# The decoding's loads and stores moved from SyncE's queue to ScalarE's, with other tile counts

## The chip, the cores and the metric

The kernel runs on one core of one Trainium2 chip. The metric is the device time of one execution in microseconds (us). The kernel before was timed three times; the median is 1176.22 us.

## What is computed

Three stages follow each other. The first is causal attention with a decay per position, for 4 batches of 8 heads, 576 positions and 64 channels each:

```python
scores = scale * np.matmul(q, k.transpose(0, 1, 3, 2))
log_f = np.log(np.clip(f, 0.0001, 1.0))
cum = np.cumsum(log_f, axis=-1)
decay = cum[:, :, :, None] - cum[:, :, None, :]
scores = np.where(causal, -1000000000.0, scores + decay)
attn = np.exp(scores - np.max(scores, axis=-1, keepdims=True))
attn = attn / (np.sum(attn, axis=-1, keepdims=True) + 1e-09)
x = np.matmul(attn, v)
```

The heads side by side give 2304 tokens of 512 channels. Two layers of three weights each follow, with 1536 inner channels: `x1 = ((x @ w_a) * (x @ w_b)) @ w_out`, and then, after a normalization of x1 by its root mean square and a gain, `(silu(xn @ w_gate) * (xn @ w_val)) @ w_out2`. The weights are given in double precision.

## The kernel before

**The tiling.** The tokens are cut into four chunks, one for each batch; a chunk has two column halves of 256 to 320 tokens. Eight phases (`PHASES`, line 33) run a layer on a chunk. A phase has 36 weight granules (24 of the two input weights, 12 of the output weight); a granule is 128 x 512 weights, and for each half it gives one block of 12 matmuls (lines 584 to 586), since each weight and each activation is held as a high and a low part and three products are added up. A block of 288 columns takes about 1.6 us.

**The decoding.** The first time that a granule is used (`weights`, line 478), its 64-bit words are loaded into a tile `raw` (512 KB, line 509); ScalarE or GpSimd takes the upper word into `w32` (lines 514 and 516), VectorE fixes two bit fields (lines 520 and 526) and joins them (line 530, the last reader of `raw`), ScalarE makes the high part (line 485, `high`), GpSimd the low part (line 488, `low`), and the result, a tile `w` of 512 KB, is used and also stored into `wd` in device memory (line 535, `save`). There are 72 granules. Whenever a granule is used again, the stored form is loaded (line 494, 251 times). Before the change there are two `raw` tiles, so a raw load waits until the join of the granule two places earlier is done.

**The attention** is woven between the weight blocks. For each pair of heads `head` (line 1049) loads q, k, two rows each of decay sums (`aux`) and the values (`vr`, two loads); that is twelve transfers a pair. Then come the scores (lines 1108 and 1130), their maximum with the mask on VectorE (line 770), exp on ScalarE (line 777), transposes on TensorE (line 813), the copy of the transposed tile `pt` on ScalarE (line 1197), and the value products (line 1168).

**What sets the order.** `Plan` records every step as a node with an engine, a cost, a priority and its dependencies, simulates the engines (`order`, line 213), and writes the instructions in the order of its simulated starts. On the chip every engine runs its own list strictly in that order, each instruction with its waits. All transfers before the change are issued by SyncE (`SP`), whose list is one queue; a transfer that must wait for its tile holds up those behind it. The tiles rotate: a tile of a kind with n buffers waits until the users of the one n places earlier are done. The gate tiles are `a` (line 605), also used for the squares and for the outputs.

Of the kernel before, what the change touches and what calls it, by code (L numbers as in the profile page):

```python
# [13 lines left out]
I64 = mybir.dt.int64  # L14
# [44 lines left out]
QUIET = 9000  # L59

NORM_AT, NORM_STEPS = 6, (6, 10)
W_BUFS, W32_BUFS, A_BUFS, BP_BUFS = 5, 3, 4, 4
S_BANKS, T_BANKS, PV_BANKS, M_BANKS = 2, 1, 1, 4
P_BUFS, PT_BUFS = 3, 4


def mm(n):
# [9 lines left out]
def turn_cost(k, n):  # L77

    return k * (57 if n <= 64 else 109) - (50 if n > 64 else 0)


def act(n, psum=False):
    return (51 if psum else 93) + n / 1.2
# [60 lines left out]
class Plan:  # L144
# [7 lines left out]
    @staticmethod  # L152
    def latency(a, b):

        if a == SP:
            return 980
        if a == b:
            return {PE: 0, POOL: 0, DVE: 128}.get(a, 128)
        return 200 if a == PE else 230 if b == PE else 170 if b == POOL else 140

    def __init__(self):
        self.nodes, self.writer, self.readers, self.rings = [], {}, {}, {}
# [50 lines left out]
    def order(self):  # L213
# [23 lines left out]
        while len(done) < len(self.nodes):  # L237
            best = None
            for e, ns in cand.items():
                pick = None  # L240
                for n in ns:
                    t = max(free[e], n.ready)
                    if shared(n, e):
                        t = max(t, port[other[e]])
                    if pick and (t, n.prio) >= pick[0]:
                        continue
                    ok = True
                    if isinstance(n.eng, tuple):
                        ends_ = [
                            max(free[x], n.ready, port[other[x]] if shared(n, x) else 0) + c + (PEN if x == DVE else 0)  # L250
                            for x, c in zip(n.eng, n.cost)
                        ]
                        ok = ends_[n.eng.index(e)] == min(ends_)
                    for b in n.allocs if ok else ():
                        ring, i = self.rings[b.tag], turn[b.tag]
                        if ring[i] is not b:
                            ok = False
                            break
                        if i >= b.bufs:
                            ends = [u.end for u in ring[i - b.bufs].users]  # L260
                            if None in ends:
                                ok = False
                                break
                            t = max(t, max(u.end + self.latency(u.eng, n.eng) for u in ring[i - b.bufs].users))
                    if not ok:
                        continue
                    key = (t, n.prio)
                    if pick is None or key < pick[0]:
                        pick = key, n
                if pick and (best is None or pick[0][0] < best[0][0]):  # L270
                    best = *pick, e
# [14 lines left out]
            n.end = free[n.eng] = t + cost * (2 if n.eng == PE and t < self.COLD else 1)  # L286
            if shared(n, n.eng):
                port[n.eng] = n.end + 60
            if n.eng == SP:
                n.end = dma_free = max(t + 1150, dma_free) + n.bytes / 360  # L290
            done.append(n)
            for o in n.outs:
                o.waiting -= 1
                to = o.eng[0] if isinstance(o.eng, tuple) else o.eng
                o.ready = max(o.ready, n.end + self.latency(n.eng, to))
                if not o.waiting:
                    offer(o)
        done.sort(key=lambda n: n.start)
# [4 lines left out]
class Kernel:  # L303
# [119 lines left out]
    def weave(self):  # L423
# [10 lines left out]
        for p in range(np_):  # L434
            self.T.append([t])
            c = PHASES[p][1]
            for x, s in zip(extra[p], (s for _, subs in self.steps(p) for s in subs)):
                t += 12 * mm(size(c, s)) + x
                self.T[-1].append(t)
        self.x_parts, self.ab_blocks, self.decoded = {}, {}, set()  # L440
        self.plan_boot()
        self.op(
            DVE, dve2(128),
# [28 lines left out]
    def source(self, m, j):  # L472
        if j < 2 * FT:
            return self.w[m][j % 2][j // 2]
        j -= 2 * FT
        return self.w[m][2][j // 3, j % 3]

    def weights(self, m, j, t, start=0):
# [19 lines left out]
        self.decoded.add((m, j))  # L498


        raw = self.tile([128, 512], "raw", 2, I64)
        i32 = self.tile([128, 512], "w32", W32_BUFS, I32)

        def words(dtype, n):
            x = raw.tile.bitcast(dtype).rearrange("p (n t) -> p n t", t=n)
            return [x[:, :, i] for i in range(n)]

        def load(x):
            nc.sync.dma_start(x, self.source(m, j))

        def rebase(by, x):
            x, y = x.bitcast(F32), words(F32, 2)[1]
# [19 lines left out]
            )  # L532

        def save():
            nc.sync.dma_start(self.wd[m][j], flat(w.tile))

        op(SP, 480, load, writes=[raw], prio=t - 14000, nbytes=524288, start=start)
        op((ACT, POOL), (act(512) + 50, pool1(512)), rebase, reads=[raw], writes=[i32], prio=t - 8500)
        op(DVE, dve_words(512), last_bits, writes=[raw], prio=t - 8000, port=True)
        op(DVE, dve_words(512), sign, writes=[raw], prio=t - 7500, port=True)  # L540
        op(DVE, dve(512), join, reads=[raw], writes=[i32], prio=t - 7000, port=True)
        op(ACT, act(512), high, reads=[i32], writes=[(w, 0)], prio=t - 6000)
        op(POOL, pool2(512), low, reads=[i32, (w, 0)], writes=[(w, 1)], prio=t - 5500)
        op(
            SP, 480, save, reads=[(w, 0), (w, 1)], writes=[("wd", m, j)], prio=t - 4000, nbytes=524288,
        )
        return w

# [500 lines left out]
    def head(self, c, h, q0, t, sf):  # L1049
# [16 lines left out]
        top, dt, aux, at = (66, F32, self.aux32, (0, 1)) if sf else (68, F32R, self.aux, (0, 2))  # L1066
        qb, kb = (self.tile([top, S], x + "b", 2, dt) for x in "qk")
        qr, kr = (qb, kb) if sf else (self.tile([64, S], x, 1) for x in ("qr", "kr"))
        vr = self.tile([128, 5, D], "vr", 4)
        load(256 * (S - q0), lambda: qr.tile[0:64, q0:], self.qT[g, :, q0:], writes=[(qr, 0)], dt=15000)  # L1070
        load(147456, lambda: kr.tile[0:64], self.kT[g], writes=[(kr, 0)], dt=15000)
        for x, i in zip((qb, kb), at):
# [177 lines left out]
```

## Time and profile before

| | us |
|---|---|
| median of three runs (1173.39 to 1176.52) | 1176.22 |
| profiled execution | 1176.44 |
| its span, first to last instruction | 1174.6 |
| TensorE busy | 1146.0 |
| VectorE / ScalarE / GpSimd busy | 635.3 / 498.7 / 193.8 |

The span is one execution seen by the profiler. PE is TensorE, DVE VectorE, ACT ScalarE, POOL GpSimd, SP SyncE; SPq is SyncE's queue, where a row is the issue of a transfer and not the transfer itself. The granted clock is the share of 2.4 GHz at which TensorE was allowed to run; at the lower level of 1.2 GHz it reads 0.5, and a stretch that holds both reads in between. Idle time is put down to what ended it.

### The profile page before, as it was taken

What the parts mean: (1) busy time and instruction counts of PE and PEld (TensorE: products, weight loads), DVE (VectorE), ACT (ScalarE), POOL (GpSimd) and SP (SyncE); (2) the same over time, 40 slices, a digit from 0 to 9 for tenths busy, and PEclk for the clock granted to TensorE, in tenths of its full rate; (3) what the DMA queues carried; (4) which work ended last, traced back from release to release, by engine and by line L of the source; (5) the groups of instructions that cost most, each with busy time, mean ns of one, the idle gap of its engine ahead of it and who ended that gap; (6) DMA issues with size and microseconds to landing.
All of it is one profiled execution on the core that took longest, in us unless ns stands there. A gap on an engine that the chain in (4) does not pass through costs nothing.

```text
span 1174.6 us, 22748 instructions
## 1 busy us (share of the span) xinstructions
PE 1146.0 (98%) x8752; PEld 1087.2 (93%) x8752; DVE 635.3 (54%) x1654; ACT 498.7 (42%) x1272; POOL 193.8 (17%) x198
## 2 busy tenths in 40 slices
PE   8999999999899999999999999999999999999998
PEld 7666889989789999998999999999999999999998
DVE  7988857878886348897233148632132057303420
ACT  7676556656554445545223244533222134202220
POOL 2323304442323020444100010110000000000000
PEclk9999999999889999999999999999999999999999
DMA  7677686578499454567755444444555455565553
GB/s 200 237 246 257 235 316 212 198 237 320 147 335 323 146 158 139 201 225 248 235 172 159 144 155 148 137 149 152 176 172 166 161 163 165 171 200 169 164 170 119
DMA packets 76800, 229.81 MB, mean 196 GB/s; under 512 B 11444, under 2 KB 22212, under 8 KB 76660
## 3 DMA queue, kind: packets, MB, share of 16 engines
q1 hardware_dynamic: 76692, 228.36, 59.0%
q8 instruction: 69, 1.13, 0.4%
q14 instruction: 39, 0.32, 0.1%
HBM read 185.19 MB, written 43.13 MB: 194 GB/s over the span
## 4 chain that ended last, share of the span: by engine, by line
PE 72%; DVE 5%; DMA 4%; ACT 2%; issue 1%; POOL 1%; SPq 0%; ACTq 0%; POOLq 0%; DVEq 0%
PE m L584 22%; PE m L586 22%; PE m L585 21%; PE pv L1168 2%; PE t L813 2%; PE s L1108 2%; DMA raw<-wv 1%; DVE raw L526 1%; DVE w L530 1%; DMA w<-wd 1%; DMA raw<-wg 1%; DVE raw L520 1%; DMA raw<-wo 1%; PE s L1130 1%; DVE P L770 1%
## 5 line engine op out<-in xcount | busy, mean ns | idle before, releaser
L584 PE MATMUL m<-x,w 128*128 128x288 f32 (+2 forms) x1536 | 467.6, 304 | 4.0 <-DMA w<-wd 4.0
L586 PE MATMUL m<-x,w 128*128 128x288 f32 (+2 forms) x1536 | 456.6, 297 | 0.5 <-POOL w L488 0.5
L585 PE MATMUL m<-x,w 128*128 128x288 f32 (+2 forms) x1536 | 455.7, 297 | 0.0
L584 PEld LDWEIGHTS m<-x,w 128*128 128x128 f32 x1536 | 291.7, 190 | 11.6 <-DMA w<-wd 5.0
L585 PEld LDWEIGHTS m<-x,w 128*128 128x128 f32 x1536 | 291.8, 190 | 1.9 <-issue 1.0
L586 PEld LDWEIGHTS m<-x,w 128*128 128x128 f32 x1536 | 291.4, 190 | 1.1 <-POOL w L488 0.9
L584 PE MATMUL m<-g,w 128*128 128x288 f32 (+2 forms) x768 | 230.9, 301 | 0.0
L586 PE MATMUL m<-g,w 128*128 128x288 f32 (+2 forms) x768 | 227.1, 296 | 2.2 <-POOL w L488 2.2
L585 PE MATMUL m<-g,w 128*128 128x288 f32 (+2 forms) x768 | 226.5, 295 | 0.0
L626 DVE TENSOR_TENSOR a<-m,a 128x288 f32<-128x288 f32 (+2 forms) x192 | 88.0, 459 | 141.1 <-PE m L586 132.7
L642 ACT ACTIVATE g<-a 128x288 fp32r<-128x288 f32 (+2 forms) x192 | 84.9, 442 | 173.9 <-DVE a L626 173.5
L584 PEld LDWEIGHTS m<-g,w 128*128 128x128 f32 x768 | 144.7, 188 | 2.4 <-issue 2.1
L586 PEld LDWEIGHTS m<-g,w 128*128 128x128 f32 x768 | 144.4, 188 | 2.6 <-POOL w L488 2.6
L585 PEld LDWEIGHTS m<-g,w 128*128 128x128 f32 x768 | 144.7, 188 | 0.2
L608 ACT ACTIVATE a<-m 128x288 f32<-128x288 f32 (+2 forms) x192 | 78.2, 407 | 133.2 <-PE m L586 132.9
L488 POOL TENSOR_TENSOR w<-w,w 128x512 fp32r<-128x512 f32 x72 | 98.2, 1365 | 183.2 <-ACT w L485 157.7
L645 DVE TENSOR_TENSOR g<-a,g 128x288 fp32r<-128x288 f32 (+2 forms) x185 | 95.2, 515 | 59.5 <-ACT g L642 59.2
L777 ACT ACTIVATE P<-P,mn 128x512 f32<-128x512 f32 (+4 forms) x128 | 76.4, 598 | 57.4 <-DVE mn L770 56.4
L615 DVE SCALAR_TENSOR_TENSOR a<-a,m 128x288 f32<-128x288 f32 (+1 forms) x96 | 43.3, 454 | 96.8 <-ACT a L608 96.6
L770 DVE CUSTOM_DVE_ANT_0 P<-s,mask 128x512 f32<-128x512 f32 (+4 forms) x128 | 62.6, 501 | 42.2 <-PE s L1108 34.1
L1197 ACT ACTIVATE pt<-t 128x512 f32<-128x512 f32 (+4 forms) x144 | 63.9, 444 | 50.1 <-PE t L813 49.8
L813 PE MATMUL t<-ident,P 128*128 128x128 f32 (+1 forms) x376 | 67.7, 281 | 7.8 <-ACT pt L1197 5.2
(106 smaller groups left out, 1170.5 us busy)
## 6 DMA issues: line engine op xcount, KB each, us to landing
w<-wd SPq DMA_DIRECT2D x251, 512.0 KB
wd<-w SPq DMA_DIRECT2D x72, 512.0 KB
raw<-wo SPq DMA_DIRECT2D x24, 512.0 KB
raw<-wa SPq DMA_DIRECT2D x12, 512.0 KB
raw<-wb SPq DMA_DIRECT2D x12, 512.0 KB
raw<-wg SPq DMA_DIRECT2D x12, 512.0 KB
raw<-wv SPq DMA_DIRECT2D x12, 512.0 KB
vr<-vA SPq DMA_DIRECT2D x32, 128.0 KB
```

What stands on the lines that cost most here:

```text
L488: nc.gpsimd.tensor_tensor(out=w.tile[:, 1, :], in0=i32.tile.bitcast(F32), in1=w.tile[:, 0, :].bitcast(F32), op=ALU.subtract)
L584: nc.tensor.matmul(o, w.tile[:, 0, wc], xh, start=kt == 0, stop=False)
L585: nc.tensor.matmul(o, w.tile[:, 0, wc], xl, start=False, stop=False)
L586: nc.tensor.matmul(o, w.tile[:, 1, wc], xh, start=False, stop=kt == last)
L608: ACT, act(n, 1), lambda x: nc.scalar.activation(x[:, :n], acc.tile[:, :n], func, scale=scale),
L626: nc.vector.tensor_tensor(out=a.tile[:, :n], in0=acc.tile[:, :n], in1=a.tile[:, :n], op=ALU.mult)
L642: nc.scalar.activation(out(0), x(), AF.Copy, **({} if scale is None else {"scale": scale}))
L645: self.engine(by).tensor_tensor(out=out(1), in0=x(), in1=out(0).bitcast(F32), op=ALU.subtract)
L770: nc.vector.tensor_tensor_reduce(out=p.tile[:n, i * w : i * w + w], in0=s[i].tile[:n, :w], in1=masks[i][:n], scale=-0.125, scalar=mn.tile[ ...
L777: nc.scalar.activation(o, o, AF.Exp, bias=mn.tile[:n, len(s) - 1 : len(s)], scale=-1.0, accum_out=x[:n])
L813: nc.tensor.transpose(ps.tile[:w, c : c + n], p.tile[:n, i * 128 : i * 128 + w], self.ident[:n, :n])
L1197: ACT, act(m, 1), lambda *_: self.nc.scalar.activation(x.tile[:rows, :m], ps.tile[:rows, :m], AF.Copy),
```

## The change

The 72 raw loads and the 72 stores are issued by ScalarE instead of SyncE. In the planner they are nodes of ScalarE with a cost of 120 ns (`DMA_ACT`), and their end is still reckoned as a transfer's. A raw load is made dependent on the `high` step of the granule three places earlier, which is on the same engine and comes after the join. There are three `raw` tiles instead of two, and three instead of four of `a`, `pt` and `vr`. As the planner's inputs differ, it writes other orders for all engines. The lines of the changed file are 8 to 12 higher: 502 is 494 of before, 518 is 509, 544 is 535, 493 is 485, 596 to 598 are 584 to 586, 620 is 608, 789 is 777, 800 is 788, 825 is 813, 1074 is 1062, 1120 is 1108, 1180 is 1168, 1209 is 1197.

```diff
-W_BUFS, W32_BUFS, A_BUFS, BP_BUFS = 5, 3, 4, 4
+RAW_BUFS, W_BUFS, W32_BUFS, A_BUFS, BP_BUFS = 3, 5, 3, 3, 4
...
-P_BUFS, PT_BUFS = 3, 4
+P_BUFS, PT_BUFS, VR_BUFS = 3, 3, 3
...
+DMA_ACT = 120
...
+    @staticmethod
+    def source(n):
+        return SP if n.bytes else n.eng
...
-            t = max(t, max(u.end + self.latency(u.eng, n.eng) for u in ring[i - b.bufs].users))
+            t = max(t, max(u.end + self.latency(self.source(u), n.eng) for u in ring[i - b.bufs].users))
...
-            if n.eng == SP:
+            if n.bytes:
                 n.end = dma_free = max(t + 1150, dma_free) + n.bytes / 360
...
-                o.ready = max(o.ready, n.end + self.latency(n.eng, to))
+                o.ready = max(o.ready, n.end + self.latency(self.source(n), to))
...
-        self.x_parts, self.ab_blocks, self.decoded = {}, {}, set()
+        self.x_parts, self.ab_blocks, self.decoded, self.highs = {}, {}, set(), []
...
-        raw = self.tile([128, 512], "raw", 2, I64)
+        raw = self.tile([128, 512], "raw", RAW_BUFS, I64)
...
         def load(x):
-            nc.sync.dma_start(x, self.source(m, j))
+            nc.scalar.dma_start(x, self.source(m, j))
...
         def save():
-            nc.sync.dma_start(self.wd[m][j], flat(w.tile))
-
-        op(SP, 480, load, writes=[raw], prio=t - 14000, nbytes=524288, start=start)
+            nc.scalar.dma_start(self.wd[m][j], flat(w.tile))
+
+        op(
+            ACT, DMA_ACT, load, writes=[raw], prio=t - 14000, nbytes=524288, start=start,
+            after=self.highs[-RAW_BUFS:][:1] if len(self.highs) >= RAW_BUFS else [],
+        )
...
-        op(ACT, act(512), high, reads=[i32], writes=[(w, 0)], prio=t - 6000)
+        self.highs.append(op(ACT, act(512), high, reads=[i32], writes=[(w, 0)], prio=t - 6000))
...
         op(
-            SP, 480, save, reads=[(w, 0), (w, 1)], writes=[("wd", m, j)], prio=t - 4000, nbytes=524288,
+            ACT, DMA_ACT, save, reads=[(w, 0), (w, 1)], writes=[("wd", m, j)], prio=t - 4000, nbytes=524288,
         )
...
-        vr = self.tile([128, 5, D], "vr", 4)
+        vr = self.tile([128, 5, D], "vr", VR_BUFS)
```

**SyncE, at granule 12 of the second chunk's phase** (`wd0_12` is its stored form; qr and kr are head loads, raw a granule to decode). Before:

```order
L1062 DMA qb803_4162<-aux_136 4x576
L1062 DMA kb804_4183<-aux_136 4x576
L1062 DMA qb810_4190<-aux_136 4x576
L1062 DMA kb811_4194<-aux_136 4x576
L1062 DMA qr812_4272<-qT 64x576
L1062 DMA kr813_4276<-kT 64x576
L509 DMA raw1122_4302<-wv 128x512
L494 DMA w1109_4305<-wd0_12_150 128x1024
```

Now:

```order
L1074 DMA qb803_4159<-aux_136 4x576
L1074 DMA kb804_4171<-aux_136 4x576
L1074 DMA qb810_4195<-aux_136 4x576
L1074 DMA kb811_4200<-aux_136 4x576
L502 DMA w1109_4210<-wd0_12_150 128x1024
L1074 DMA qr812_4285<-qT 64x576
L1074 DMA kr813_4305<-kT 64x576
L502 DMA w1117_4308<-wd0_13_151 128x1024
```

The load of granule 12 stood behind qr, kr and a raw load; now it stands ahead of qr and kr, and the raw load is gone from this queue.

**TensorE, a little later** (s are scores of a head pair, t transposes of its first softmax). Before:

```order
L1108 MATMUL s827_4406<-ka809_4185,qa808_4165 128x128
L1108 MATMUL s827_4406<-kb804_4183,qb803_4162 128x128
L1108 MATMUL s831_4413<-ka816_4323,qa815_4309 128x128
L1108 MATMUL s831_4413<-kb811_4194,qb810_4190 128x128
L1108 MATMUL s840_4427<-ka809_4185,qa808_4165 128x256
L1108 MATMUL s840_4427<-kb804_4183,qb803_4162 128x256
L1108 MATMUL s844_4432<-ka816_4323,qa815_4309 128x256
L1108 MATMUL s844_4432<-kb811_4194,qb810_4190 128x256
L813 MATMUL t824_4453<-ident_96,P819_4402 128x128 x4
```

Now:

```order
L1120 MATMUL s827_4498<-ka809_4186,qa808_4161 128x128
L1120 MATMUL s827_4498<-kb804_4171,qb803_4159 128x128
L1120 MATMUL s831_4504<-ka816_4369,qa815_4349 128x128
L1120 MATMUL s831_4504<-kb811_4200,qb810_4195 128x128
L596 MATMUL m1132_4515<-x100_120,w1128_4467 128x288
L597 MATMUL m1132_4515<-x110_124,w1128_4467 128x288
L598 MATMUL m1132_4515<-x100_120,w1128_4467 128x288
```

Before, eight score matmuls and then the transposes follow each other; now two weight blocks of granule 15 come after the first four (the three rows of m1132 repeat, and m1133 follows), and the loads' earlier places put six blocks of granules 12 to 14 ahead of s817, where there were two.

**ScalarE, in the first stage, at the second head pair** (`pt114` and `pt115` are copies of transposed tiles for TensorE; the names in brackets are the semaphores that an instruction waits for, DMAHW0 to 7 those of transfers). Before:

```order
L788 ACTIVATE P111_798<-P111_798,sm113_846 128x576 [waits DVE_49,Activation_49]
L485 ACTIVATE w542_880<-w32544_815 128x512 [waits DMAHW5_49,DVE_49]
L1181 ACTIVATE x000_112<-pv102_858 128x128 [waits PE_49]
L608 ACTIVATE a537_886<-m536_833 128x256
L788 ACTIVATE P124_848<-P124_848,sm126_856 128x384 [waits DVE_49,Activation_49]
L1197 ACTIVATE pt114_903<-t116_889 128x512 [waits PE_49]
L514 ACTIVATE w32553_942<-raw552_875 128x512 [waits DMAHW6_49,Pool_49]
L1197 ACTIVATE pt115_946<-t117_927 64x128 [waits PE_49]
L485 ACTIVATE w547_951<-w32549_872 128x512 [waits DMAHW7_49,DVE_49]
```

Now:

```order
L544 DMA wd0_7_145<-w547_897 128x1024 [waits DMAHW3_49,Pool_49]
L518 DMA raw561_942<-wa 128x512 [waits DMAHW6_49]
L620 ACTIVATE a546_948<-m545_913 128x256 [waits PE_49]
L1209 ACTIVATE pt114_952<-t116_936 128x512 [waits PE_49]
L493 ACTIVATE w551_955<-w32553_849 128x512 [waits DMAHW0_49,DVE_49]
L800 ACTIVATE P124_926<-P124_926,sm126_931 128x384 [waits DVE_49,Activation_49]
L518 DMA raw566_982<-wb 128x512 [waits DMAHW3_49]
L1209 ACTIVATE pt115_987<-t117_967 64x128 [waits PE_49]
L789 ACTIVATE P133_984,sm135_993<-P133_984,mn134_985 128x512 [waits DVE_49]
L544 DMA wd0_8_146<-w551_955 128x1024 [waits DMAHW6_49,Pool_49]
```

Three of the moved issues stand among the softmax and decoding steps. The load `raw566` waits for DMAHW3, whose user before it is the store `wd0_7`, issued four computing steps and one load earlier, and the copy `pt115` stands behind it.

## Rows read from the trace of the kernel before

**Rows 1.** The page's parts 1 and 2: busy time by engine; granted clock in 40 slices (tenths).

```profile
PE 1146.0 (98%) x8752; PEld 1087.2 (93%) x8752; DVE 635.3 (54%) x1654; ACT 498.7 (42%) x1272; POOL 193.8 (17%) x198
...
PEclk9999999999889999999999999999999999999999
```

**Rows 2.** Busy time by stretch: us, then each engine's busy us (instructions), clock, DMA share, GB/s.

```profile
0.00:560.00 560.00, 534.47 (x4054) 481.77 (x4055) 424.59 (x1102) 324.03 (x831) 177.56 (x178) 0.98 0.68 231
```

**Rows 3.** The same view in stretches of 10 us.

```profile
110.00:120.00 10.00, 9.19 (x59) 5.90 (x57) 9.02 (x25) 6.87 (x20) 3.16 (x3) 0.83 0.67 234
...
130.00:140.00 10.00, 9.65 (x60) 8.50 (x61) 7.81 (x18) 4.67 (x11) 3.23 (x3) 0.83 0.59 221
...
300.00:310.00 10.00, 7.88 (x70) 7.47 (x68) 7.69 (x20) 6.62 (x17) 5.74 (x8) 0.99 0.45 133
310.00:320.00 10.00, 7.45 (x35) 7.02 (x35) 8.34 (x20) 3.59 (x9) 0.36 (x1) 0.67 0.34 115
320.00:330.00 10.00, 7.81 (x41) 5.97 (x42) 7.62 (x23) 6.05 (x17) 2.54 (x2) 0.50 0.81 279
```

**Rows 4.** TensorE in order of time: start us, length us, line, out<-in, [idle before <-releaser].

```profile
311.15 0.61 PE L584 MATMUL m<-x,w 128*128 128x288 f32 x1 [3.28 <-DMA w<-wd]
...
319.00 0.33 PE L1108 MATMUL s<-ka,qa 128*128 128x128 f32 x1 [0.90 <-DVE mn L770]
...
322.80 1.12 PE L813 MATMUL t<-ident,P 128*128 128x128 f32 x4 [0.82 <-ACT P L788]
...
327.95 0.61 PE L584 MATMUL m<-x,w 128*128 128x288 f32 x1
```

**Rows 5.** SyncE's queue in order of time (same columns).

```profile
298.26 0.29 SPq L1062 DMA_DIRECT2D kb<-aux  x1
303.14 0.47 SPq L1062 DMA_DIRECT2D qr<-qT  x1
304.40 0.47 SPq L1062 DMA_DIRECT2D kr<-kT  x1
305.40 0.36 SPq L509 DMA_DIRECT2D raw<-wv  x1
305.82 0.42 SPq L494 DMA_DIRECT2D w<-wd  x1
...
320.52 0.33 SPq L509 DMA_DIRECT2D raw<-wg  x1
320.90 0.90 SPq L494 DMA_DIRECT2D w<-wd  x2
```

**Rows 6.** VectorE in order of time, around 300 to 326 us (same columns).

```profile
304.70 0.68 DVE L530 SCALAR_TENSOR_TENSOR w<-w,raw 128x512 int32<-128x512 int32 x1
...
319.80 0.69 DVE L530 SCALAR_TENSOR_TENSOR w<-w,raw 128x512 int32<-128x512 int32 x1
```

**Rows 7.** TensorE's waits: engine line <- releaser: us in total, times, longest us.

```profile
PE t L813 <- ACT pt L1197: 5.2, 8, 1.5
PE m L584 <- DMA w<-wd: 4.0, 3, 3.3
PE m L586 <- POOL w L488: 2.7, 3, 1.4
```

**Rows 8.** SyncE's issues of the stores (line 535): durations in ns, min/median/max.

```profile
L535 SPq DMA_DIRECT2D wd<-w x72: 319/320/1170, 21.0 to 560.2; - x72
```

**Rows 9.** SyncE's waits (columns as TensorE's waits).

```profile
SPq L535 <- POOL w L488: 105.3, 57, 6.0
...
SPq L494 <- DMA wd<-w: 7.9, 3, 4.8
```

**Rows 10.** ScalarE in order of time (columns as TensorE's).

```profile
309.87 0.66 ACT L514 ACTIVATE w<-raw 128x512 f32<-128x512 f32 x1 [1.64 <-DMA raw<-wv]
```

**Rows 11.** ScalarE's groups up to 560 us: busy us, mean ns, idle before.

```profile
L485 ACT ACTIVATE w<-w 128x512 fp32r<-128x512 f32 x72 | 45.1, 627 | 22.7 <-DVE w L530 13.5 <-PE m L586 5.9 <-issue 1.6
```

**Rows 12.** GpSimd's groups (same columns).

```profile
L488 POOL TENSOR_TENSOR w<-w,w 128x512 fp32r<-128x512 f32 x72 | 98.2, 1365 | 183.2 <-ACT w L485 157.7 <-issue 10.5 <-PE pv L1168 4.5
```

## The prediction

> **What bounds the kernel now.** I read the page's busy shares first: TensorE works 1146.0 of the 1174.6 us of the span (98%), ScalarE 42%, GpSimd 17% [rows 1]. So almost all of the time is matmul work that the change does not touch, and it can only win or lose where TensorE stands, or where it works at the lower of its two clock levels (1.2 instead of 2.4 GHz). Next I looked where that is. All decoding lies in the first 560 us; there TensorE is idle for 560 - 534.5 = 25.5 us [rows 2]. In windows of 10 us one place stands out [rows 3]: from 300 to 330 us TensorE works 7.88, 7.45 and 7.81 of 10, so it is idle for 6.9 us, and its clock falls to 0.67 and 0.50. At half speed this costs another 7.45 x 0.33 + 7.81 x 0.50 = 6.4 us. The place costs 13.3 us in all.
>
> Then I asked the timelines why. TensorE stood 3.28 us for a stored weight tile, until 311.15 [rows 4]. SyncE had issued that load only at 305.82, because its queue runs in order [rows 5]: after 298.26 it stood for two head loads (qr, kr) and then for a raw load, which went out at 305.40, as the last read of the old raw tile, a join, ended at 305.38 (304.70 + 0.68) [rows 6]. The weight load waited for none of this; it stood behind it. The same again later: the raw load of 320.52 follows a join that ends at 320.49 (319.80 + 0.69), and two weight loads come out right behind it, at 320.90 [rows 5, 6]. Meanwhile TensorE has only scores, transposes and value products, each of which waits for VectorE or ScalarE (0.90, 0.82 us and smaller), and no weight block between them until 327.95 [rows 4].
>
> The sum is made against the profiled execution: 1176.44 us, that is the span of 1174.6 and 1.84 around it, and 0.2 us above the median of 1176.22.
>
> **What goes.** (a) The load of granule 12 stands ahead of qr, kr and every raw load in the new order of SyncE. The stand of 3.28 us and the slow matmuls after it (7.45 x 0.33 = 2.5) should go: 5.8 us. Ends: 0, if something else is late there, and 5.8.
> (b) The rest of the place is 13.3 - 5.8 = 7.5 us. In the new order of TensorE weight blocks stand between the scores of this head pair and its transposes. But VectorE, 76% busy up to 560 us (424.59 of 560 [rows 2]), still does the softmax, so not all of it is covered. I take three fifths, 4.5 us; ends 0 and 7.5.
> (c) TensorE waited 2.7 us for GpSimd's low parts of decoded weights [rows 7]. A third raw tile lets a load start one granule earlier. I take 1.5; ends 0 and 2.7.
> Together 11.8 us, with ends 0 and 16.0.
>
> **What comes.** (d) The issues. 144 transfers (72 loads, 72 stores) leave SyncE, which loses 144 x 0.32 = 46 us of issuing [rows 8] that nobody waits for by itself, and join ScalarE's stream. The trace shows no transfer issued there: between 0 and 0.32 us each, 0 to 46 us of that engine. ScalarE is idle for 236 of the first 560 us [rows 2], so only an issue in front of a copy that TensorE waits for counts. TensorE waits 5.2 us in 8 places for the copy of a transposed tile [rows 7]; some eight such places, at 0.12 us (SyncE's 0.32 is the nearest row, but ScalarE has idle time to hide part), give 1.0. Ends 0 and 5.
> (e) All 72 stores wait for GpSimd. On SyncE that took 105.3 us, 57 times [rows 9], with weight and head loads behind it. On ScalarE the store is placed after the step it needs, so only the planner's error is left: the low part takes 1.365 us [rows 12] where the planner reckons 1.227, so 0.14 us each, 10 us in all if nothing hides it. Behind a waiting store stand exps and copies, for which TensorE waits. Nearly all lies under weight blocks; I take 0.7, ends 0 and 10.
> (f) The waits that the diff does not show. The transfers share eight completion semaphores in turn, and each issue first waits until the one eight places before it has landed. 112 of the 144 moved issues carry such a wait, now in ScalarE's queue. The order shows the shape of it: a load that needs the landing of a store which was issued only four computing steps earlier, with a copy for TensorE behind it. A transfer of this size takes 4.47 us from issue to its first reader (305.40 [rows 5] to 309.87 [rows 10]); SyncE's own waits for a store reach 4.8 [rows 9]. Four steps of at most 0.63 us [rows 11] cover 2.5, so ScalarE stands for up to 2.0 us; the steps' own waits shorten this, and I take 1.2. The burst of twelve transfers of a head pair laps the eight semaphores, so I count one such wait for three of the four pairs of the first stage, where matmul work is scarce: 3.6 us. Ends: 0, and 16 pairs x 2.0 = 32.
> (g) The clock. Two windows before 140 us show 0.83, that is 3.4 us at the lower level, after idle time well under 1 us in the same window [rows 3]; such a piece costs 10 x 0.17 = 1.7 us. New stands of ScalarE should bring one more: 1.7. Ends 0 and 5.1.
> (h) One tile less of a, pt and vr: nothing. A gate tile is free again two weight blocks (3.2 us) before the third one in turn is wanted; pt is covered by the next unit's scores, vr by its early load. Without that cover TensorE would pay a wait as in (d).
> Together 7.0 us. The sum: 1176.44 - 11.8 + 7.0 = **1171.6 us**, 0.4% faster.
>
> **The rivals.** B, the stands of SyncE only change their name. With three vr tiles the value loads must wait for an earlier pair's last product, in SyncE's queue and with weight loads behind them, and raw loads now run beside the weight loads on the same transfers' bandwidth. Then only (a) is won: 1176.44 - 5.8 + 7.0 = 1177.6. For it: the queue still stands mostly for TensorE. Against it: the new order keeps these loads behind the weight load of rows 5.
> A rule of the Trainium skill speaks for B ("DMA: Bandwidth & Descriptors", section "Issuing engines are not separate DMA queues"): transfers started by different engines run on the same 16 DMA engines and interleave, so a second issuing engine only saves the issue time. By that rule alone, (a) to (c) would be nothing and the time 1176.4. The rows bear on it: the weight load of rows 5 was late by its issue, not by its transfer, so the rule does not reach (a).
> C, slower: ScalarE's in-order queue becomes what TensorE waits for. Its place is the first 150 us, where ScalarE feeds every transpose; its price is (f) in five bursts at 2.0 us, 10.0, with (d) at 2.0, (e) at 0.7 and two clock pieces, 3.4: 16.1 us against 11.8, so 1180.7. It decides once the costs pass 11.8 + 3.5 = 15.3. For it: 112 semaphore waits in a queue that had none of this kind. Against it: ScalarE's 236 idle us.
> D, ScalarE takes the moved work in its idle time: only (d) and (e) are paid, 1176.44 - 11.8 + 1.7 = 1166.3.
> That the change does not do what it says can be left out: the built order has all 144 transfers on ScalarE.
>
> **How the numbers follow.** Under about 0.3% (3.5 us) a measurement of this kernel cannot tell a difference. Forecast A 0.42, its own range 1168 to 1176 from the halves of (b) and (f), 0.27 of it faster and 0.15 the same; B 0.22 (0.19 same, 0.03 slower); C 0.20, slower; D 0.16, faster. So faster 0.43, same 0.34, slower 0.23. The range of 1163.5 to 1182.0 takes in A, B, most of D and more than half of C.
>
> **What would show it.** (a): near granule 12's load SyncE goes on without the 7 us between 298 and 306, and no row of 3.28 us for a stored weight tile. (b): the clock stays near 1.00 between 300 and 330 us. (d): ScalarE's issue rows, their length. (e), (f): ScalarE's waits for a transfer, and TensorE's wait for pt copies, 5.2 us now, growing to about 10; far more than that is C. The forecast is wrong if the windows from 55 to 150 us lose more than 300 to 330 us gain, or if weight loads are still what TensorE waits for longest.

## The result, and the profile after

The changed kernel takes 1184.66 us (median of five runs, 1183.47 to 1185.93), the kernel before 1176.22: a ratio of 1.0082, interval 1.0053 to 1.0111. A second set of its runs, with the kernel before beside it on one chip (run e5 below), gave 1.0111 (1.0067 to 1.0156). So it is slower by about 1%, where 0.4% faster was forecast. The profiled execution took 1185.25 us with a span of 1183.4, 8.8 more than before.

TensorE's own work is the same: 1145.1 us busy, where it was 1146.0 [rows 1]. From the page of the kernel after, the busy times:

```profile
PE 1145.1 (97%) x8766; PEld 1087.8 (92%) x8766; DVE 626.2 (53%) x1650; ACT 502.6 (42%) x1280; POOL 196.4 (17%) x194
```

Up to 560 us TensorE works 524.85 us, 9.6 less than before [rows 2], as all of the work has moved later by that much. Stretches show where (us, busy us of PE, PEld, DVE, ACT and POOL with instructions, clock, DMA share, GB/s), first of the kernel before, then of the changed one:

```profile
0.00:55.00 55.00, 48.90 (x339) 38.41 (x339) 45.19 (x147) 38.73 (x106) 18.73 (x26) 0.97 0.69 217
55.00:150.00 95.00, 89.53 (x654) 69.66 (x653) 81.33 (x204) 61.25 (x153) 30.37 (x27) 0.96 0.74 248
...
300.00:330.00 30.00, 23.14 (x145) 20.45 (x144) 23.65 (x61) 16.26 (x41) 8.64 (x10) 0.72 0.54 176
330.00:560.00 230.00, 225.61 (x1763) 216.74 (x1763) 161.88 (x393) 116.55 (x291) 67.56 (x66) 1.00 0.65 220
```

```profile
0.00:560.00 560.00, 524.85 (x3985) 475.24 (x3986) 404.26 (x1051) 318.56 (x809) 177.03 (x167) 0.98 0.69 230
...
0.00:55.00 55.00, 45.83 (x307) 37.16 (x307) 40.00 (x123) 34.19 (x94) 17.97 (x24) 0.94 0.69 209
55.00:150.00 95.00, 84.94 (x631) 65.72 (x632) 75.77 (x209) 64.92 (x162) 31.78 (x28) 0.98 0.77 260
...
110.00:120.00 10.00, 5.22 (x53) 4.56 (x51) 6.23 (x17) 5.03 (x14) 1.10 (x2) 0.95 0.91 267
...
300.00:330.00 30.00, 28.05 (x221) 26.62 (x220) 26.49 (x66) 19.82 (x47) 12.65 (x12) 1.00 0.64 232
330.00:560.00 230.00, 220.39 (x1692) 211.96 (x1692) 157.32 (x375) 110.47 (x274) 64.56 (x59) 0.99 0.65 220
```

The place of the forecast is healed: from 300 to 330 us TensorE is idle for 1.9 us instead of 6.9, and the clock is 1.00 instead of 0.72. But TensorE is idle for 3.1 us more up to 55 us, the boot, for 4.6 us more from 55 to 150 us, most of it from 110 to 120 us (4.8 us, where it was 0.8), and for 5.2 us more from 330 to 560 us. TensorE's waits name the causes (line <- releaser: us, times, longest):

```profile
PE t L825 <- ACT pt L1209: 10.3, 9, 2.8
PE bm L892 <- DMA bk<-kT: 4.6, 1, 4.6
PE s L1142 <- DVE kb L1070: 3.6, 1, 3.6
PE pv L1180 <- ACT pt L1209: 3.5, 4, 1.3
PE m L596 <- DMA w<-wd: 2.5, 3, 1.0
PE t L825 <- DVE P L803: 2.0, 1, 2.0
PE m L598 <- POOL w L496: 1.5, 2, 1.2
```

Two of them are shorter: the waits for stored tiles (4.0 before) and for GpSimd's low parts (2.7) [rows 7]. Longer are the waits for the copies of transposed tiles (`pt`; for the transposes alone 5.2 before [rows 7] and 10.3 now, 13.8 with those of the value products) and the one in the boot, 2.3 before and 4.6 now. Two single waits for VectorE are new, both after 330 us: 2.0 us at 385.08 and 3.6 us for `kb` at 544.84. They vary: in a second profile of the same program (e5) the first is 1.9 us and the second 0.6. The experiments below do not explain them.

ScalarE in order of time shows how a copy comes late (ACTq is its queue, where a row is the issue of a transfer):

```profile
105.46 0.34 ACTq L518 DMA_DIRECT2D raw<-wb  x1
...
110.04 0.19 ACT L789 ACTIVATION_READ_ACCUMULATOR P<-P,mn 128x1 f32 x1
112.56 0.33 ACTq L544 DMA_DIRECT2D wd<-w  x1
112.93 0.49 ACT L1209 ACTIVATE pt<-t 128x384 f32<-128x384 f32 x1 [2.70 <-DMA raw<-wb]
...
115.68 0.33 ACTq L544 DMA_DIRECT2D wd<-w  x1
116.06 0.66 ACT L523 ACTIVATE w<-raw 128x512 f32<-128x512 f32 x1 [1.62 <-DMA vr<-vB]
...
118.62 0.49 ACT L1209 ACTIVATE pt<-t 128x384 f32<-128x384 f32 x1
```

The store at 112.56 could not be issued before the raw load of 105.46 had landed, 7 us after its issue. It does not need that load: the two have the same completion semaphore. Behind it stands the copy that TensorE needs. At 115.68 the same happens with a value load of SyncE; the copy of 118.62 comes behind that, a further issue and six computing steps. TensorE, at the same time:

```profile
113.48 0.55 PE L825 MATMUL t<-ident,P 128*128 128x128 f32 x3 [1.93 <-ACT pt L1209]
...
119.17 1.11 PE L825 MATMUL t<-ident,P 128*128 128x128 f32 x4 [2.84 <-ACT pt L1209]
```

Counted over the whole trace, from the end of ScalarE's step or issue before to the start of the issue, and put down to the semaphore that rose last, there are 9 stands of over 0.1 us for a completion semaphore, 8.1 us in all, 8 of them before 120 us; and 19 in which a store waits for GpSimd's low part, 13.1 us in all. The expectations below that speak of 8.0 and 15.7 us counted otherwise. SyncE's queue stands longer too, for stores that are now issued elsewhere, where it was 7.9 us before [rows 9]:

```profile
SPq L502 <- DMA wd<-w: 41.7, 12, 7.1
```

The boot, SyncE before and ScalarE after, and then TensorE before and after:

```profile
8.07 0.42 SPq L509 DMA_DIRECT2D raw<-wa  x1
8.54 0.44 SPq L509 DMA_DIRECT2D raw<-wb  x1
```

```profile
4.36 0.41 ACTq L518 DMA_DIRECT2D raw<-wa  x1
...
4.80 0.45 ACTq L518 DMA_DIRECT2D raw<-wb  x1
```

```profile
11.39 1.55 PE L880 MATMUL bm<-bk,bq 128*128 128x128 f32 x8 [2.32 <-DMA bk<-kT]
```

```profile
13.72 2.90 PE L892 MATMUL bm<-bk,bq 128*128 128x128 f32 x8 [4.64 <-DMA bk<-kT]
```

On SyncE the first two raw loads stood behind the boot's loads and the store of `aux`. On ScalarE nothing is ahead of them, so they start 3.7 us earlier, before the load of the keys `bk` that SyncE issues at 4.34 us is done, and TensorE gets the keys 2.3 us later.

### The profile page after: what moved, and what is told of

Same layout as the page of the kernel before. It is cut to its first block, busy times and chain, and to the rows that moved or that the text cites. A ratio compares the mean times of both kernels' runs of the same rounds, so it can differ in the third digit from the quotient of the medians.

```text
span 1183.4 us, 22660 instructions
## 1 busy us (share of the span) xinstructions
PE 1145.1 (97%) x8766; PEld 1087.8 (92%) x8766; DVE 626.2 (53%) x1650; ACT 502.6 (42%) x1280; POOL 196.4 (17%) x194
## 3 DMA queue, kind: packets, MB, share of 16 engines
q10 hardware_dynamic: 20736, 75.51, 18.2%
## 4 chain that ended last, share of the span: by engine, by line
PE 68%; DVE 6%; DMA 5%; ACT 2%; issue 1%; POOL 1%; ACTq 0%; SPq 0%; DVEq 0%; POOLq 0%
PE m L596 21%; PE m L598 20%; PE m L597 20%; PE pv L1180 2%; PE t L825 2%; DMA raw<-wg 2%; PE s L1120 2%; DMA raw<-wo 1%; DVE raw L535 1%; DVE w L539 1%; DMA raw<-wv 1%; DVE raw L529 1%; PE s L1142 1%; DVE g L657 1%; ACT P L789 0%
## 5 line engine op out<-in xcount | busy, mean ns | idle before, releaser
L496 POOL TENSOR_TENSOR w<-w,w 128x512 fp32r<-128x512 f32 x72 | 101.9, 1420 | 180.2 <-ACT w L493 149.4
L657 DVE TENSOR_TENSOR g<-a,g 128x288 fp32r<-128x288 f32 (+2 forms) x182 | 91.1, 501 | 60.2 <-ACT g L654 59.6
L825 PE MATMUL t<-ident,P 128*128 128x128 f32 (+1 forms) x376 | 67.6, 281 | 13.2 <-ACT pt L1209 10.3
(105 smaller groups left out, 1172.2 us busy)
```

Of the source, the lines that this page charges most:

```text
L496: nc.gpsimd.tensor_tensor(out=w.tile[:, 1, :], in0=i32.tile.bitcast(F32), in1=w.tile[:, 0, :].bitcast(F32), op=ALU.subtract)
L657: self.engine(by).tensor_tensor(out=out(1), in0=x(), in1=out(0).bitcast(F32), op=ALU.subtract)
L825: nc.tensor.transpose(ps.tile[:w, c : c + n], p.tile[:n, i * 128 : i * 128 + w], self.ident[:n, :n])
```

## The experiments

Theory 1: ScalarE's queue stands at the moved issues, and its copies come late. Theory 2: the planner's new orders and the missing tiles make the loss. Theory 3: a part of it is the boot. Theory 4, added later: raw loads on a second queue share the transfers' bandwidth with the head loads. In e1 to e3, e6, e7, e9, e10, e13 and e14 the order was frozen: the planner still reckons as before the edit, and only the queue of an instruction is another, or one is added, so that only the lists of these two queues change. A count of stands is made as above. Every ratio is to the kernel before, measured beside it.

**e1, all 144 back on SyncE, order frozen.**

```diff
-            nc.scalar.dma_start(x, self.source(m, j))
+            nc.sync.dma_start(x, self.source(m, j))
...
-            nc.scalar.dma_start(self.wd[m][j], flat(w.tile))
+            nc.sync.dma_start(self.wd[m][j], flat(w.tile))
```

> The order of every engine stays that of the changed kernel; only the 144 issues go back to SyncE's queue, at the places that the planner gave them. Theory 1 (ScalarE's queue stands at the moved issues and is late with the copies of transposed tiles): TensorE's waits for pt copies fall from 13.8 us (10.3 and 3.5) to 7 or less, its wait at 13.7 us in the boot from 4.6 to about 2.3, as the two raw loads are behind the boot's loads again; SyncE stands for the stores again. Time 1173 to 1178. Theory 2 (the planner's new orders and the tiles that were taken away make the loss): the time stays within 1183 to 1187, and the waits at 385 and 545 us stay.

0.9972 (0.9944 to 0.9999), with 6.7 us of waits for `pt` copies and 1.5 us in the boot. The queue alone makes 1.1 to 1.4% between this and the changed kernel; the orders and the tiles are worth a small gain. Theory 2 falls.

**e2, the first two raw loads on SyncE; e3, the stores on SyncE; e7, both; e6, all raw loads on SyncE and the stores on ScalarE** (order frozen in all four; e2's edit, the others are lines of e1):

```diff
+        first = len(self.decoded) <= 2
...
-            nc.scalar.dma_start(x, self.source(m, j))
+            (nc.sync if first else nc.scalar).dma_start(x, self.source(m, j))
```

> Only the first two raw loads go back to SyncE, behind the boot's loads and the store of aux; every other row of every engine stays. Theory 3 (part of the loss is the boot: two early loads of 512 KB on a second queue run beside the boot's loads of q and k): TensorE's wait for bk falls from 4.6 to about 2.3 us, and the time by 2 to 4 us, to 1181 to 1183. If the boot's loss is hidden later, the wait falls and the time stays at 1184 to 1185.

> The order of every engine stays that of the changed kernel; the 72 stores are issued by SyncE, the 72 raw loads stay on ScalarE. In the trace of the changed kernel ScalarE's longest stands (2.4 and 1.3 us at 112 to 116, 2.6 at 228, 1.5 at 264 us) are ahead of stores. Theory 1: pt waits of TensorE fall from 13.8 to 8 us or less, time 1176 to 1180. If the loads make it (their issues and their waits for completion semaphores), pt waits stay over 12 us and the time at 1183 to 1186. Theory 2: time 1183 to 1187.

> The order of every engine stays that of the changed kernel; the 72 raw loads are issued by SyncE, the 72 stores stay on ScalarE. Theory 1 in the form that the stores make ScalarE stand (15.7 of its 23.6 us of stands longer than 0.1 us are ahead of stores that wait for GpSimd): the time lies 2 to 4 us above the kernel with all 144 on SyncE, 1172 to 1176; TensorE's waits for pt copies stay over 8 us, the boot's wait for bk is 1.5. Theory 1 in the form that the loads do it (their early start and their waits): as the kernel with all on SyncE, 1168 to 1171.

> The order of every engine stays that of the changed kernel; the stores and the first two raw loads are issued by SyncE, the other 70 raw loads by ScalarE. Moving the first two gave about 6 us, moving the stores about 3. If the parts add up: 1175 to 1176, and what is left above the kernel with all 144 on SyncE (5 us) is the price of 70 raw loads on ScalarE. If the boot and the stores are the whole price, 1168 to 1171.

e2: 1.0031 (1.0004 to 1.0057). e3: 1.0052 (1.0024 to 1.0079). e7: 1.0020 (0.9994 to 1.0046). e6: 0.9953 (0.9925 to 0.9981). Two expectations were wrong. In e3 I took the stores for the worse half, as most of ScalarE's stands are ahead of them; moving them gave only 0.3 to 0.6%, hardly clear of the noise, although the waits for `pt` copies fell from 13.8 to 5.1 us. And e6, with all 72 stores on ScalarE, is as quick as anything measured here, though ScalarE stands 16.8 us for GpSimd there, none of it for a completion semaphore. Its longest, at 221.70:

```profile
221.70 0.33 ACTq L544 DMA_DIRECT2D wd<-w  x1
222.07 0.68 ACT L523 ACTIVATE w<-raw 128x512 f32<-128x512 f32 x1 [3.08 <-POOL w L496]
```

Behind it stands a decoding step, not a copy, and TensorE has no wait there. So waits of the stores for GpSimd cost nothing that shows here. The raw loads do: e6 to e2 is 0.8% for the 70 later ones, and e2 to the changed kernel 0.5 to 0.8% for the first two. e1 to e7 prices the 70 at 0.5%, with the stores on SyncE. Each of these differences has an interval of 0.4 to 0.5% to either side.

The stand of 110 to 120 us is not the semaphores' alone. In e6, where ScalarE waits for none, TensorE waits 4.10 us for a copy at the very transposes that wait 2.84 us at 119.17 in the changed kernel, because a decoding step that waits for a late raw load is ahead of the copy. ScalarE, then TensorE:

```profile
109.31 0.66 ACT L523 ACTIVATE w<-raw 128x512 f32<-128x512 f32 x1 [2.16 <-DMA raw<-wa]
...
109.97 0.48 ACT L1209 ACTIVATE pt<-t 128x384 f32<-128x384 f32 x1
```

```profile
110.51 0.90 PE L825 MATMUL t<-ident,P 128*128 128x128 f32 x3 [4.10 <-ACT pt L1209]
```

In all, e6 has 6.6 us of `pt` waits and e2 has 13.3.

In e2 TensorE's boot wait is down to 1.76 us, and it reaches the scores that stood at 38.69 us in the changed kernel 4.4 us earlier:

```profile
38.69 1.38 PE L1142 MATMUL s<-kb,qb 66*128 66x288 f32 x4 [0.94 <-DVE x L956]
```

```profile
10.84 1.55 PE L892 MATMUL bm<-bk,bq 128*128 128x128 f32 x8 [1.76 <-DMA bk<-kT]
...
34.30 2.07 PE L1142 MATMUL s<-kb,qb 66*128 66x288 f32 x4 [0.63 <-DVE x L956]
```

**e5, the changed kernel again.**

> The changed kernel itself, unchanged, beside the other runs of this call as their measure. 1184.7 us and a ratio of 1.0082 were measured; both theories expect 1182 to 1187 again.

1190.64 us, 1.0111, above what was expected. Its runs spread from 1179 to 1197, and the profiled one, 1179.3, is the lowest; so in what follows a time is read from the medians and a mechanism from a profile.

**e4, the tile counts alone; e8, fewer tiles with two raw buffers.** In e4 loads and stores are nodes of SyncE at 480 ns again. e8 is the kernel before with

```diff
-W_BUFS, W32_BUFS, A_BUFS, BP_BUFS = 5, 3, 4, 4
+W_BUFS, W32_BUFS, A_BUFS, BP_BUFS = 5, 3, 3, 4
...
-P_BUFS, PT_BUFS = 3, 4
+P_BUFS, PT_BUFS = 3, 3
...
-        vr = self.tile([128, 5, D], "vr", 4)
+        vr = self.tile([128, 5, D], "vr", 3)
```

and e4 is the changed kernel with

```diff
-            ACT, DMA_ACT, load, writes=[raw], prio=t - 14000, nbytes=524288, start=start,
+            SP, 480, load, writes=[raw], prio=t - 14000, nbytes=524288, start=start,
...
-            ACT, DMA_ACT, save,
+            SP, 480, save,
```

and with `nc.sync` in both functions, without the dependence on `high`.

> The queue move is undone in the planner too: loads and stores are nodes of SyncE with 480 ns as before; three raw tiles and three of a, pt and vr stay, so this is the tile counts alone, with the orders that the planner writes for them. Term (h) of the prediction was nothing and term (c) a gain of 1.5: 1174 to 1177 by it. Theory 2 with the tiles as its cause: 1180 or more, with TensorE's waits for the exponentials' copies, for kb or P longer than before. Theory 1: within 3 us of the kernel before.

> The kernel before with three instead of four of a, pt and vr and with two raw tiles as it had; nothing else. With three raw tiles as well it took 0.995 of the kernel before. If the third raw tile made that gain: 1176 to 1180, ratio 1.000 to 1.005. If the planner's new order made it and the raw tile is worth nothing: ratio 0.993 to 0.998. If fewer tiles cost something of themselves: over 1.005, with TensorE's waits for pt or vr longer.

e4: 0.9950 (0.9924 to 0.9976). e8: 0.9978 (0.9959 to 0.9998). The missing tiles cost nothing. Whether the third raw tile or the order makes the gain of e4 is not settled: the intervals meet. Three raw tiles beside the old numbers of the others were not run.

**e9, the boot by itself:** in the kernel before, with its order frozen, the first two raw loads are issued by ScalarE (the edit of e2 turned round).

> The kernel before, with the order of every engine as it was; only the first two raw loads are issued by ScalarE. Theory 3 (on a queue of their own these two run beside the boot's loads of q and k instead of behind them): TensorE's wait for bk in the boot grows from 2.3 to 4.5 us or more, all that follows in the boot shifts with it, and the time is 4 to 8 us over the kernel before, ratio 1.003 to 1.007. If the later part of the first stage takes the shift back: ratio 0.999 to 1.002.

1.0031 (1.0007 to 1.0056): 3.6 us, just under the 4 to 8 that I expected, and the interval does not quite exclude that the shift is taken back later (up to 1.002). The boot's wait grows from 2.3 us, though not to 4.5:

```profile
PE bm L880 <- DMA bk<-kT: 4.1, 1, 4.1
```

**e10, small stores; e13, small steps; e14, small stores in the first 130 us only.** All start from e6; at the place of each later raw load ScalarE does one thing more, with no use for the result.

```diff
-            nc.scalar.dma_start(x, self.source(m, j))
+            nc.sync.dma_start(x, self.source(m, j)); k = len(self.ks); self.ks.append(0); k > 1 and nc.scalar.dma_start(self.dum[k : k + 1, :], self.ident.bitcast(F32)[0:1, :])
```

Their line numbers are one higher than the changed kernel's; `self.dum` is a scratch array in device memory, `self.ks` counts the loads. In e13 the added step is `nc.scalar.activation(self.junk, self.ident, AF.Copy)`; in e14 the condition is `1 < k < 24`.

> The kernel with the raw loads on SyncE and the stores on ScalarE (ratio 0.9953), and at the place of each of the 70 later raw loads ScalarE also issues a store of 512 bytes to a scratch row. So ScalarE pays the issue and the waits for completion semaphores of a raw load there, and the raw load itself stays in SyncE's queue. The matching kernel with these 70 raw loads on ScalarE has 1.0031. Theory 1 (what costs is ScalarE's queue): ratio 1.001 to 1.004, and waits of TensorE for pt copies over 11 us, as with the raw loads. Theory 4 (what costs is that 512 KB loads on a second queue run beside the head loads and share the transfers' bandwidth with them): ratio 0.994 to 0.998, pt waits 6 to 8 us.

> As the kernel with 70 small stores at the places of the later raw loads (ratio 1.0028), but each is a computing step of ScalarE on 128 x 128 values that nobody reads (about 0.25 us, as long as the small store's issue of 0.24), with no completion semaphore. If the time that the issues occupy ScalarE is the cost: ratio 1.001 to 1.004. If their waits for semaphores are the cost (in the changed kernel 8 stands, 8.0 us): ratio 0.994 to 0.998, as without them.

> As the kernel with 70 small stores on ScalarE, but only the 22 that lie before about 130 us. If the first stage is the place (rival C's place), where ScalarE feeds every transpose and head loads lap the eight semaphores: ratio 1.001 to 1.004 as with all 70. If the cost is spread evenly: about a third of 0.75%, 0.997 to 0.999.

e10: 1.0028 (1.0011 to 1.0046), all of the 0.8%, though no large transfer was moved: for the later loads theory 4 is not needed. e13: 0.9957 (0.9933 to 0.9981), nothing. Its step takes even longer than the issue it stands for, the first row from e13, the second from e10:

```profile
L519 ACT ACTIVATE junk<-ident x70: 292/298/322, 9.7 to 538.3; 128x128 f32<-128x128 f32 x70
```

```profile
L519 ACTq DMA_DIRECT2D dum<-ident x70: 220/242/487, 9.3 to 534.9; - x70
```

So it is not the time of the issue. What the small store has and the small step has not is a transfer with its completion semaphore. e10 has a stand for one in its trace, here ScalarE, then TensorE, then the clock:

```profile
69.14 0.35 ACTq L545 DMA_DIRECT2D wd<-w  x1
71.93 0.24 ACTq L519 DMA_DIRECT2D dum<-ident  x1
72.22 0.38 ACT L621 ACTIVATE a<-m 128x256 f32<-128x256 f32 x1 [2.65 <-DMA kb<-kT]
...
74.23 0.58 ACT L1210 ACTIVATE pt<-t 128x512 f32<-128x512 f32 x1
```

```profile
74.86 0.66 PE L826 MATMUL t<-ident,P 128*128 128x128 f32 x4 [3.00 <-ACT pt L1210]
```

```profile
70.00:80.00 10.00, 6.80 (x44) 4.30 (x43) 5.66 (x10) 5.20 (x11) 3.75 (x3) 0.78 0.74 218
80.00:90.00 10.00, 10.00 (x41) 6.79 (x40) 6.72 (x21) 4.42 (x11) 1.32 (x1) 0.71 0.67 246
```

The small store waits 2.4 us for a key load of SyncE that had its semaphore before, the copy behind it is late, TensorE stands 3.00 us, and then works partly at its lower level: 6.80 x 0.22 + 10.00 x 0.29 = 4.4 us more. At the same place of e13 ScalarE goes from the store at 69.29 to the next computing step without a stand:

```profile
69.29 0.33 ACTq L545 DMA_DIRECT2D wd<-w  x1
69.66 0.31 ACT L519 ACTIVATE junk<-ident 128x128 f32<-128x128 f32 x1 [0.27 <-issue]
69.88 0.36 ACT L621 ACTIVATE a<-m 128x256 f32<-128x256 f32 x1
```

But in e13, too, TensorE then stands for a copy, and its clock falls as much:

```profile
72.69 0.66 PE L826 MATMUL t<-ident,P 128*128 128x128 f32 x4 [1.67 <-ACT pt L1210]
```

```profile
70.00:80.00 10.00, 8.00 (x40) 4.11 (x36) 6.90 (x13) 5.98 (x14) 2.98 (x3) 0.72 0.87 295
80.00:90.00 10.00, 10.00 (x49) 7.62 (x48) 6.46 (x20) 5.93 (x16) 2.00 (x2) 0.77 0.46 162
```

That is 8.00 x 0.28 + 10.00 x 0.23 = 4.5 us. So the stand of the small store is worth the 1.3 us between 3.00 and 1.67, and the 4.4 us are not its price. Nor do the whole traces show the 0.7%. I expected more than 11 us of waits for `pt` copies in e10; they are 5.4 us, in e13 7.1 and in e6 6.6. ScalarE's stands for completion semaphores are 3.0 us in e10 and 1.4 in e13. And the small stores take places in the turn of the semaphores, so that SyncE's transfers wait for other ones as well: SyncE's waits for transfers, added up, are 65.2 us in e10 and 50.7 in e13. The runs show that a small transfer in ScalarE's queue costs what the raw load there costs, and a computing step does not; that it does so by the waits for semaphores, and in which queue, is argued by exclusion.

e14: 1.0001 (0.9976 to 1.0026), between its two expectations. The 22 issues of the first 130 us bring 0.5 of the 0.8%, but with 0.4% of noise to either side this cannot be told from their third or from all. That the first stage is the main place is not shown.

**e11, e12, e15, e16, versions that the planner orders anew.** e11: of e4's edit the raw loads' half, with the stores on ScalarE. e12:

```diff
-DMA_ACT = 120
+DMA_ACT = 340
```

e15: that, and e2's edit with the first two raw loads as SyncE's nodes of 480 ns. e16: e11 and e12 together.

> The changed kernel with the raw loads as SyncE's nodes of 480 ns again; the stores stay ScalarE's nodes, three raw tiles and three of a, pt and vr stay, and the planner writes its orders for that. In the order of the changed kernel this assignment gave 0.9953, with everything on SyncE and planned so 0.9950. All theories: under the kernel before, ratio 0.992 to 0.998; under 0.992 it would be the best version of the study.

> The changed kernel, with the planner reckoning 340 ns for an issue on ScalarE instead of 120, as the trace measured (333 to 339). If the wrong price made the loss, by placing copies for TensorE behind issues: ratio under 1.004 and pt waits under 10 us. If the loss is in waits and transfers that the planner does not see (theories 1, 3 and 4): ratio 1.006 to 1.013.

> The changed kernel with the planner's price of 340 ns (alone 1.0008) and with the first two raw loads as SyncE's nodes behind the boot's loads (worth 0.3 to 0.7% so far). If the two parts add up: ratio 0.994 to 0.998, that is, no loss is left and the move costs nothing once both are mended. If the later loads still cost: 0.999 to 1.003.

> Raw loads as SyncE's nodes, stores on ScalarE at a price of 340 ns, three raw tiles, three of a, pt and vr: the same as the replanned version with 120 ns (0.9959) but for the price. If the price matters for the stores as well: 0.990 to 0.994. If stores on ScalarE are free in any case: 0.994 to 0.998.

e11: 0.9959 (0.9934 to 0.9984). e12: 1.0008 (0.9991 to 1.0025). e15: 0.9958 (0.9935 to 0.9981). e16: 1.0000 (0.9980 to 1.0020), outside of what I expected. e12 came out as expected for a wrong price, with 4.0 us of waits for `pt` copies: with all 144 transfers still on ScalarE, most of the loss is gone in another order. e12 to e15, 0.5%, is the boot and a new order in one. But e11 and e16 differ by 0.4% in nothing but the planner's price, and e16 should have been the better one. So an order written anew brings a chance of its own of some 0.4%, and it stays open how much of e12's gain is the right price. What e15 does show is that the move need not cost: in its order ScalarE still stands for completion semaphores in 5 places, 7.9 us in all, as long as in the changed kernel, but TensorE's waits for `pt` copies are 6.6 us.

No version beats the kernel before by much. e6 and e4, with the raw loads on SyncE and three raw tiles, are both at 0.995.

## Why the prediction was wrong

**The step that failed** is the price of ScalarE's queue: (f), the waits for the eight completion semaphores, with the clock (g) at 3.6 + 1.7 = 5.3 us, in costs of 7.0 us together. Between e1 and the changed kernel the queue, the boot included, costs 1.1 to 1.4%, 13 to 16 us. Two more steps failed beside it: the boot is missing from the sum, and the gain of 11.8 us was taken for the whole kernel's, of which 3 to 6 us are left.

- (a) and (b), 5.8 and 4.5: came true in their place. The waits and the lower clock from 300 to 330 us cost 13.3 us before and 1.9 now. That gain is not the kernel's: with the queue undone, e1, e4 and e6 are 3 to 6 us faster. The part that the clock had in it, 6.4 us, is not kept in the changed kernel's order: the median granted clock over a kernel's executions is 0.990 in e1 and 0.991 in e6, and 0.991 in the kernel before beside each (e4, in another order, has 0.993).
- (c), 1.5: the wait for low parts fell from 2.7 [rows 7] to 1.5.
- (d), 1.0: nothing measurable. The issues take 333 to 346 ns on ScalarE (medians by tensor), hardly more than SyncE's 320 [rows 8], and e13's 70 steps of 298 ns cost nothing.
- (e), 0.7: nothing measurable, in spite of 16.8 us of stands (e6). The upper end of 10 was far too high: behind the longest of them TensorE has no wait.
- (f) and (g): ScalarE's stands are 8.1 us instead of 3.6, and e10 against e13, 0.71%, prices a transfer in the place of each of the 70 loads at 8.4 us. I counted three stands by the bursts of head loads; but the semaphores go round over all transfers, so a store also waits for a raw load of ScalarE's own that takes 7 us. Nor is a stand paid at its own length: 9.6 us of them in e2 cost 0.8%, 3.0 us in e10 cost 0.7%, and 7.9 us in e15 nothing. The clock moves with the loss: its median is 0.991 in e6 and 0.9905 in e13, but 0.984 in e10, and 0.986 and 0.983 in the two sets of the changed kernel. By that (an estimate), 0.007 of 1176 us is 8.2 us in e10, where (g) has 1.7. It is not all: at a granted clock of 0.990 and 0.991 two executions of e10 took 1174.7 us, and five of e13 1170.4 to 1172.2.
- The boot: I did not ask what the first two raw loads were behind in SyncE's list, and what they would start beside. It costs 3.6 us (e9) to 9 us (e2 to the changed kernel, 0.8%). A rule of the Trainium skill ("DMA: Bandwidth & Descriptors", section "Issuing engines are not separate DMA queues") says that transfers of different issuing engines share the 16 DMA engines and interleave. The prediction weighed it against (a) alone; the boot is where the traces agree with it: two loads from another queue, and the keys land 2.3 us later.
- (h), nothing: right (e8).

Rival C had the right side, ScalarE's queue, at 1180.7. Its costs of 16.1 us are near the 13 to 16 that were measured, by luck, as it has no boot in them; what kept it under the result is the gain of 11.8 that it shares with the forecast. Its place, the first 150 us, has part of the loss. The chain of runs from e6 (0.9953) over e2 (1.0031) to the changed kernel prices the later 70 loads at 0.8% and the first two at 0.5 to 0.8%; added by themselves elsewhere, 70 small transfers come to 0.7% (e10 against e13) and the first two loads to 0.3% (e9). Rival B's stands of SyncE came, 41.7 us for stores instead of 7.9 [rows 9], but TensorE waits only 2.5 us for stored tiles. Of the forecast's own signs one spoke: `pt` waits of 13.8 us are "far more than" 10. The other did not: from 55 to 150 us 4.6 us of idle time are added at a higher clock, less than 300 to 330 us gain. The boot and the time after 330 us, which no sign covered, add 8.3 us of idle time.

Not settled: what the third raw tile is worth, how much of the loss another order or the right price in the planner (e12) can avoid, why TensorE's clock is lower in the slower versions, and what makes the waits after 330 us. That a transfer in ScalarE's queue costs is shown by small stores in the place of the loads; that its completion semaphore is the reason is not shown. Giving the moved transfers semaphores of their own was not tried.

## What to carry to other kernels

Moving a transfer to a computing engine's queue moves all that its issue waits for, also the wait that the code does not show, for the transfer that had the same completion semaphore before: list those waits and find what stands behind each, since their sum is no price. A gain at one place of a trace is not yet the kernel's: the next stop and the clock can take it back. Ask also what a moved transfer was queued behind: here its old place had kept two loads back by 3.7 us, and the keys landed 2.3 us earlier for it. And when a planner orders the work, freeze the order for an experiment: new orders alone differ by 0.4% here.

## What the runs showed that was not expected

A wait of ScalarE's queue is nearly free or expensive by what is behind it: 16.8 us of stands for GpSimd cost nothing in e6 and 7.9 us for completion semaphores nothing in e15, while 70 issues of 242 ns, in whose trace two stands of 3.0 us in all are for semaphores, cost 0.7% in e10. A single profile does not show such a loss. e10's profiled span is 8.1 us longer than e6's (1174.4 and 1166.3) with only 2 us more of idle time (20.2 and 18.2, all gaps of TensorE over 0.03 us added up), so most of the rest goes with the clock, 0.984 and 0.991. But e13's profiled execution, the slowest of its 12, has a clock of 0.984 and a span of 1176.7 us as well, and e13 is as quick as e6. One kernel's executions differ by as much as the loss, and only the medians of 12 tell the versions apart.
